# Hourglass attention and a quick-GELU MLP on one core: batch 0's values loaded by halves of the heads, the second half as fp32 over SyncE's queue

## The chip, the cores and the metric

The kernel runs on one core of a Trainium2 chip. The metric is the device time of one execution in microseconds; smaller is better. A core has five engines that run side by side, each with its own instruction stream in program order: TensorE (PE, matmuls, with its weight loads as PEld), VectorE (DVE), ScalarE (ACT), GpSimd (POOL) and SyncE (SP, which here only issues DMAs). They meet through semaphores. DMAs are issued by POOL (queue 0, which can also convert fp32 to bf16 on the way), by SP (queue 1) and once by ACT (queue 10).

## The reference

Two attentions over the same q, k, v (8 batches, 8 heads, 576 positions, head size 64), added, then an MLP with x * sigmoid(1.702 x):

```python
q_d = q.reshape(B, H, Sd, factor, D).mean(axis=3)      # factor 4; k_d, v_d alike
out_d = sm_attn(q_d, k_d, v_d)                         # softmax attention on 144 positions
out_up = np.repeat(out_d, factor, axis=2)
mask = np.abs(pos[:, None] - pos[None, :]) < factor    # local attention, 7 keys wide
out_local = np.matmul(attn, v)
x = (out_up + out_local).transpose(0, 2, 1, 3).reshape(B * S, H * D)   # 4608 x 512
h = x @ w_in                                           # 512 -> 2048
out = (h * (1.0 / (1.0 + np.exp(-1.702 * h)))) @ w_out # 2048 -> 512
```

## The kernel before, in words

The order of every engine's work is written out by hand (`manual_schedule`): instructions stand on their engine in the order in which the program issues them, and only the waits are added for it.

The MLP runs over nine groups of 512 tokens. For a group, `mm1` makes sixteen 128-row pieces (ffc 0 to 15) of h, each of four matmuls with w_in (`hps_mm`, L738), and ACT turns each into gT by Silu (L749). `mm2` multiplies gT by w_out (L808), four 128-token tiles of sixteen matmuls each, and stores. In group 0 the order of `mm2` is cut so that the late pieces of w_out come late: tiles 2, 3, 0, 1 with f 0 to 7 first (32 matmuls), then tile 0 with f 8 to 11 and f 12 to 15, and so on.

The attention of batch g + 1 is done inside group g, as steps between the matmuls of the MLP. `POS_G[0]` says ahead of which matmul of group 0 each step of batch 1 stands (numbers from 16 on count `mm2`'s matmuls), `VDP_0` the same for the selection matmuls of batch 1.

Batch 0 has nothing to hide behind, so its attention is the kernel's start. "qd" is one of two quads of four heads, "hp" one of four pairs of heads. In order:

- POOL loads k and q of both quads as bf16 (`load_1`, L183), then values: `load_vb` (L214) loads, for chunk i of five and each half of the partitions, 64 rows of all eight heads into `vbs[0]`, eight DMAs of 64 KB for chunks 0 to 3. Chunk 4 comes as fp32 by SP and ACT at the very start (`load_v`, L203) and ACT converts it (`prep_v`, L325).
- DVE transposes k and q (L261) and sums them by four positions (L304); POOL sums one of them (`pool_qk`, L315, L319). PE computes local scores (`scores`, L381, L394) and pooled ones (`scores_d`, L411); ACT takes exponents into `es` (L477) and `ed` (L483).
- `prep_vd_pe` makes the pooled values: selection matmuls (L362) with a 0/1 matrix `psel` on `vbs[0]`, all eight heads at once, fourteen of 256 columns, copied into `vd` by ACT (L371).
- `av_local0` (L499) and `av_down0` (L513, L522) are the products with the values, one pair at a time; `normalise0` on DVE (reciprocal L541, products L544 and L549) divides by the sums. Pairs 0 and 1 (the first quad) are done in two parts, pairs 2 and 3 whole (`av_whole0`).
- `turned` transposes a pair's result on PE (L564, L575) and ACT copies it into xT (L587, L591). Then the MLP's first matmuls (`part`) begin, two ffc at a time, between the transposes.
- `warm` (L606) issues matmuls without use, in gaps of PE.

POOL's stream around this matters: it holds, in order, the k and q loads of batch 0, the eight `load_vb`, w_in's first quarter, `pool_qk`, w_in's other three quarters (`load_w_in`, L237), k and q of batch 1, two pieces of w_out (`load_w_out`, L246), batch 1's values, and later the rest of w_out. A DMA issue waits for the landing of the DMA eight issues earlier, whose semaphore it takes over; POOL waits there with everything behind it.

Of the kernel before, what the change touches and what calls it, by code (L numbers as in the profile page):

```python
# [8 lines left out]
FP32 = mybir.dt.float32  # L9
# [10 lines left out]
def kernel(  # L20
# [9 lines left out]
    nc = tc.nc  # L30
    B, H, S, D = q.shape
    SD = S // 4
    HP = H // 2
    NQ = H // 4
# [6 lines left out]
    KSTART = (0, 56)  # L41
# [8 lines left out]
    ldp = ctx.enter_context(tc.tile_pool(name="loads", bufs=1))  # L50
# [11 lines left out]
    vbs = [persist.tile([128, 5, H, 65], BF16, name=f"vb{i}") for i in range(2)]  # L62
# [7 lines left out]
    PM = [psum.tile([128, 512], FP32, name=f"pm{i}") for i in range(2)]  # L70
    turn = {"m": 0}

    def pm_tile():
        turn["m"] += 1
        return PM[turn["m"] % 2]

    wz = consts.tile([128, 512], BF16, name="wz")
    wf = consts.tile([128, 512], FP32, name="wf")
# [98 lines left out]
    qf, kf, vf = {}, {}, {}  # L177
# [15 lines left out]
        load_1("k", k, kf, b, qd)  # L193
        load_1("q", q, qf, b, qd)

    def load_v(b, gate=None, chunks=range(5), queues=(nc.sync, nc.sync)):
        t = ldp.tile([128, 5, H, D], FP32, name="vf", tag="vf")
        vf[b] = t
        if gate is not None:
            gate(t[0:1, 0, 0, 0:1])  # L200
        for i in chunks:
            for par in range(2):
                queues[par].dma_start(  # L203
                    out=t[64 * par : 64 * par + 64, i],
                    in_=bass.AP(
                        tensor=v.tensor,
                        offset=v[b, 0].offset + (114 * i + KSTART[par]) * D,
                        ap=[[D, 64], [S * D, H], [1, D]],
                    ),
                )  # L210

    def load_vb(b, i):
        for par in range(2):
            nc.gpsimd.dma_start(  # L214
                out=vbs[b % 2][64 * par : 64 * par + 64, i, :, 0:D],
                in_=bass.AP(
                    tensor=v.tensor,
                    offset=v[b, 0].offset + (114 * i + KSTART[par]) * D,
                    ap=[[D, 64], [S * D, H], [1, D]],
                ),  # L220
            )

# [13 lines left out]
    def load_w_in(c, n):  # L236
        nc.gpsimd.dma_start(  # L237
            out=w_in_bf[:, :, c : c + n],
            in_=bass.AP(
                tensor=moe_w_in.tensor, offset=moe_w_in.offset + c,  # L240
                ap=[[d_ff, 128], [128 * d_ff, n_dmc], [1, n]],
            ),
        )
# [51 lines left out]
    def new_qdT(b, qd):  # L295
        t = work.tile([128, SD, 2], BF16, name=f"qdT{qd}", tag=f"qdT{qd}", bufs=1)
        qdT[b, qd] = t
        return t

    def reduce_qk(b, qd, name):  # L300
        t = kdT[qd][:, 0:SD, :] if name == "k" else new_qdT(b, qd)
        src = (kT if name == "k" else qT)[b, qd]
        with nc.allow_low_precision("the sum is rounded once, as the pairwise one is"):
            nc.vector.tensor_reduce(  # L304
                out=t, in_=src.rearrange("p (j f) a -> p j a f", f=4),
                axis=mybir.AxisListType.X, op=ALU.add,
            )

    def pool_qk(b, qd, names="kq"):
        for name, src in (("k", kT), ("q", qT)):  # L310
            if name not in names:
                continue
            sv = src[b, qd].rearrange("p (j f) a -> p j f a", f=4)
            t1 = work.tile([128, SD, 2, 2], FP32, name="pq", tag="pq")
            nc.gpsimd.tensor_tensor(  # L315
                out=t1, in0=sv[:, :, 0:2, :], in1=sv[:, :, 2:4, :], op=ALU.add
            )
            dst = kdT[qd][:, 0:SD, :] if name == "k" else new_qdT(b, qd)
            nc.gpsimd.tensor_tensor(  # L319
                out=dst, in0=t1[:, :, 0, :], in1=t1[:, :, 1, :], op=ALU.add  # L320
            )

    def prep_v(b, eng, i=slice(0, 5), h=slice(0, H)):
        cp = eng.copy if eng is nc.scalar else eng.tensor_copy
        cp(out=vbs[b % 2][:, i, h, 0:D], in_=vf[b][:, i, h])  # L325
# [22 lines left out]
    def flat(p):  # L348
        return p.rearrange("p x n -> p (x n)")

    def prep_vd_pe(b, pv, kcs=range(3), between=None):
        n = HP
        vb, vd = vbs[b % 2], vds[b % 2]
        for kc, iis in ((0, (0, 1)), (1, (1, 2, 3)), (2, (3, 4))):
            if kc not in kcs:
                continue
            c0 = 256 * (kc - kcs[0])
            if between and kc == 1:
                between()
            for i in iis:  # L360
                for j in range(2):
                    nc.tensor.matmul(  # L362
                        pv[64 * j : 64 * j + 64, c0 : c0 + D * n],
                        lhsT=psel[:, PSEL.index((i, kc)), :],
                        rhs=sub(
                            vb[:, i], 65 * (2 * j if b else j), (4 * 65, NQ), (65 * (1 if b else 2), 2), (1, D)
                        ),
                        start=(i == iis[0]), stop=(i == iis[-1]),
                        tile_position=(0, 64 * j),
                    )  # L370
        nc.scalar.copy(  # L371
            out=vd[:, kcs[0] : kcs[-1] + 1, :, 0:D],
            in_=pv[:, 0 : 256 * len(kcs)].rearrange(
                "p (k h d) -> p k h d", k=len(kcs), h=HP
            ),
        )


# [103 lines left out]
    def exp_down(qd, sd):  # L482
        nc.scalar.activation(  # L483
            out=eds[qd][:, :, 0:432], in_=sd[:, :, 0:432],
            func=AF.Exp, scale=inv_sqrt_d / 16.0,
        )
# [50 lines left out]
    def normalise0(o, y, u, parts="ab"):  # L537
        yl, yd, rc = y
        ov = o[:, :, 0:455].rearrange("p x (c e) -> p x c e", e=65)
        c0, c1 = {"a": (0, 4), "b": (4, 7), "ab": (0, 7)}[parts]  # L540
        nc.vector.reciprocal(rc[:, :, c0:c1], ov[:, :, c0:c1, 64:65])  # L541
        if "b" in parts:
            st = 2 - u
            nc.vector.tensor_tensor(  # L544
                out=yd.rearrange("p s x d -> p x s d"), in0=ov[:, :, 4 + u : 7 : st, 0:D],
                in1=rc[:, :, 4 + u : 7 : st].to_broadcast([128, 2, 2, D]), op=ALU.mult,
            )
            c1 = 6
        nc.vector.tensor_tensor(  # L549
            out=yl[:, :, c0:c1], in0=ov[:, :, c0:c1, 0:D],  # L550
            in1=rc[:, :, c0:c1].to_broadcast([128, 2, c1 - c0, D]), op=ALU.mult,
        )
# [42 lines left out]
    def sub(t, off, *dims):  # L595
        return bass.AP(
            tensor=t.tensor, offset=t.offset + off,
            ap=[list(t.ap[0])] + [list(d) for d in dims],
        )
# [3 lines left out]
    def warm(n, cols=512, t=None, z=wz):  # L603
        t = pm_tile() if t is None else t
        for _ in range(n):
            nc.tensor.matmul(  # L606
                t[:, 0:cols], lhsT=z[:, 0:128], rhs=z[:, 0:cols], start=True, stop=True
            )
# [227 lines left out]
            f()  # L836

    POS = [13, 16, 34, 44, 58, 65]
    POS_G = {0: [16, 18, 29, 42, 56, 65], 1: [13, 16, 35, 44, 58, 65]}
    VDP_0 = 34  # L840

    o, y, x = {}, {}, {}

# [9 lines left out]
    iota_psel()  # L853
    fill()
    for i in range(4):
        load_vb(0, i)
    load_w_in(0, 512)
    warm(3, z=wf)
    warm(5, 256)
    make_off()  # L860
    make_ident(di)
    make_psel()
# [8 lines left out]
    prep_1("k", 0, 1)  # L871
    prep_1("q", 0, 1)
    reduce_qk(0, 0, "q")
    pool_qk(0, 1, "q")
    reduce_qk(0, 1, "k")
    for c in range(1, 4):
        load_w_in(512 * c, 512)
    for qd in range(NQ):
        load_qk(1, qd)
    load_w_out(0)  # L880
    load_w_out(4)
    warm(2, z=wf)
    sp = scores(0, 1, PA[0:2])
    exp_local(1, sp)
    exp_down(0, scores_d(0, 0, PA[2]))
    for hp in range(4):
        o[hp] = PA[hp % 3]
        y[hp] = y_tiles0()
    warm(1, z=wf)
    prep_vd_pe(0, PM[0], range(0, 2))  # L890
    for hp in range(2):
        av_local0(hp, o[hp], range(5))
        normalise0(o[hp], y[hp], hp % 2, "a")
    prep_vd_pe(0, PM[1], range(2, 3))
    exp_down(1, scores_d(0, 1, PA[2]))
    nc.scalar.preload_act_table_set("silu_and_others")
    for hp in range(2):
        if hp == 1:
            warm(1, t=PM[0])
        av_down0(hp, o[hp])  # L900
        normalise0(o[hp], y[hp], hp % 2, "b")

    gT0 = new_gT()
    acc = PM + [PA[n][:, u, :] for n in (1, 2, 0) for u in range(2)]
# [7 lines left out]
    def av_whole0(hp):  # L912
        av_local0(hp, o[hp], range(5))
        av_down0(hp, o[hp])
        normalise0(o[hp], y[hp], hp % 2)
# [4 lines left out]
        copy_x(0, hp, PM if n is None else PA[n][:, :, 0:288])  # L920

    av_whole0(2)
    warm(1, t=PM[0])
    turned(0, None)
    av_whole0(3)
    turned(1, 1)
    part((0, 1), 0)
    part((0, 1), 1)
# [11 lines left out]
    for g in range(n_groups):  # L940
        b = g + 1
# [66 lines left out]
        if b < B:  # L1008
            pos = POS_G.get(g, POS)
            for n, f in zip(pos, attention(b)):  # L1010
                steps.setdefault(n, []).append(f)
            if g == 0:
                steps.setdefault(VDP_0, []).append(lambda: prep_vd_pe(1, flat(PA[1])))
            if g and b + 1 < B:
# [42 lines left out]
```

## Time and profile before

| What | us |
|---|---|
| Median of three runs (308.45 to 309.1) | 308.53 |
| The profiled execution | 308.58 |
| Its span, first to last instruction | 306.8 |
| PE busy in the span | 298.0 |
| PE busy from 6 to 16 us, of 10 | 8.05 |
| PE busy from 16 to 24 us, of 8 | 6.42 |
| PE busy from 24 to 58 us, of 34 | 33.93 |
| First `load_vb` issued | 4.96 |
| First MLP matmul (L738) starts | 23.18 |
| First w_out matmul (L808) starts | 39.60 |

All later numbers are microseconds from the start of the span, of this one execution. A line of the timeline has the start, the busy time, the engine, the source line, the operation, output <- input with shapes, the count, and in brackets how long the engine stood idle before and what released it. A line of the chain of waits has start, time and what ran or was waited for; "issue" is time for which the profile shows no wait. A line of the DMA issues ends with the size of one and the time from issue to landing.

### The profile page before, as it was taken

The numbers are of one execution on the slowest core, as the hardware profiler recorded it, in microseconds if no ns is written. First come the engines' busy times: TensorE is split into PE (matmuls) and PEld (weight loads), VectorE is DVE, ScalarE is ACT, GpSimd is POOL, SyncE is SP. The second block draws the span as 40 slices with busy tenths as digits, with TensorE's granted clock in tenths as the row PEclk, the third lists the DMA queues.
The fourth block names the chain that finished last, engine by engine and source line by source line (L and its number), as shares of the span: only waits on it lengthen the run. The fifth ranks groups of instructions, "written<-read, shape, count | busy, mean of one in ns | idle before, by whom it ended". The sixth has DMA issues, their size and how long they took to land.

```text
span 306.8 us, 8494 instructions
## 1 busy us (share of the span) xinstructions
PE 298.0 (97%) x3551; PEld 147.8 (48%) x3551; DVE 187.1 (61%) x354; ACT 212.9 (69%) x351; POOL 178.9 (58%) x217
## 2 busy tenths in 40 slices
PE   7879999999999999999999999999999999999995
PEld 3455455444554455445544554455444544444444
DVE  6865523966999689886897689777975430000000
ACT  5545887867887788668966896689769876226511
POOL 8855792599698968976797669845983300000000
PEclk9999999999999999999999999999999999999999
DMA  7999999999899969826973598425101110010012
GB/s 147 152 203 209 173 132 213 177 221 215 177 230 188 188 133 226 219 46 113 232 211 66 88 218 232 84 77 150 72 0 37 36 71 0 34 71 34 0 68 71
DMA packets 64662, 40.01 MB, mean 130 GB/s; under 512 B 44656, under 2 KB 56048, under 8 KB 64624
## 3 DMA queue, kind: packets, MB, share of 16 engines
q0 software_dynamic: 18352, 14.81, 35.8%
q1 hardware_dynamic: 45600, 24.46, 32.3%
q8 instruction: 28, 0.46, 0.6%
q10 hardware_dynamic: 672, 0.20, 0.3%
q14 instruction: 10, 0.08, 0.1%
HBM read 44.83 MB, written 9.44 MB: 177 GB/s over the span
## 4 chain that ended last, share of the span: by engine, by line
PE 93%; DMA 4%; issue 1%; POOL 1%; DVE 0%; ACT 0%; POOLq 0%; DVEq 0%
PE pm L808 40%; PE pm L738 36%; PE pa L681 5%; PE pa L738 5%; DMA qb<-in_q_dram 2%; DMA vb<-in_v_dram 2%; PE pa L449 2%; PE pm L824 1%; PE pa L458 1%; PE pa L394 1%; PE pa L411 0%; POOL kb L183 0%; PE pa L513 0%; PE pa L362 0%; PE pa L499 0%
## 5 line engine op out<-in xcount | busy, mean ns | idle before, releaser
L808 PE MATMUL pm<-w_out_bf,gT 128*128 128x512 bf16 x560 | 126.2, 379 | 0.0
L738 PE MATMUL pm<-xT,w_in_bf 128*128 128x512 bf16 x512 | 119.2, 379 | 0.3 <-ACT xT L591 0.3
L749 ACT ACTIVATE gT<-pm 128x512 bf16<-128x512 f32 x128 | 76.3, 598 | 42.7 <-PE pm L738 42.7
L738 PEld LDWEIGHTS <-w_in_bf 128*128 128x128 bf16 x576 | 55.6, 98 | 67.2 <-issue 0.6
L808 PEld LDWEIGHTS <-gT 128*128 128x128 bf16 x560 | 52.9, 98 | 62.2 <-issue 0.4
L699 DVE TENSOR_TENSOR xT<-pa,r 128x300 bf16<-128x300 f32 (+3 forms) x112 | 28.0, 303 | 18.6 <-ACT r L694 17.8
L787 ACT ACTIVATE osb<-pm 128x512 f32<-128x512 f32 (+2 forms) x37 | 21.5, 580 | 24.1 <-PE pm L808 21.3
L708 POOL TENSOR_TENSOR xT<-xT,ydt 128x576 bf16<-128x576 bf16 x14 | 16.2, 1173 | 31.1 <-DVE xT L699 31.1
L789 DVE TENSOR_SCALAR osb<-pm 128x128 f32<-128x128 f32 x1 | 0.3, 292 | 55.5 <-ACT osb L787 55.5
L491 DVE TENSOR_TENSOR es<-es,mask 128x600 bf16<-128x600 bf16 x28 | 19.0, 708 | 21.2 <-ACT es L477 20.9
L693 ACT ACTIVATE r<-pa 128x504 f32<-128x504 f32 (+1 forms) x42 | 24.0, 571 | 8.4 <-PE pa L681 8.4
L694 ACT ACTIVATE r<-r 128x504 f32<-128x504 f32 (+1 forms) x42 | 25.9, 616 | 1.3
L339 POOL TENSOR_TENSOR v<-v 112x512 f32<-112x512 f32 x18 | 23.5, 1306 | 0.4
L277 DVE TENSOR_REDUCE kT<-kT 32x576 bf16<-32x576 bf16 x22 | 17.5, 795 | 8.7 <-POOL odd L272 8.3
L261 DVE STREAM_TRANSPOSE kT<-kb 128x576 f32<-128x576 f32 x16 | 20.0, 1252 | 3.4 <-DMA kb<-in_k_dram 3.1
L477 ACT ACTIVATE es<-pa 128x600 bf16<-128x600 f32 x32 | 19.7, 668 | 3.4 <-PE pa L394 3.2
L261 DVE STREAM_TRANSPOSE qT<-qb 128x576 f32<-128x576 f32 x16 | 19.8, 1238 | 0.7 <-DMA qb<-in_q_dram 0.3
L738 PE MATMUL pa<-xT,w_in_bf 128*128 128x512 bf16 x64 | 20.0, 379 | 0.0
L315 POOL TENSOR_TENSOR pq<-qT 128x576 f32<-128x576 bf16 x14 | 16.0, 1145 | 6.8 <-DVE qT L277 6.6
L277 DVE TENSOR_REDUCE kT<-odd 32x576 bf16<-32x576 bf16 x22 | 17.5, 795 | 0.7
L277 DVE TENSOR_REDUCE qT<-qT 32x576 bf16<-32x576 bf16 x22 | 17.5, 795 | 0.7
L277 DVE TENSOR_REDUCE qT<-odd 32x576 bf16<-32x576 bf16 x22 | 17.4, 791 | 0.7
(107 smaller groups left out, 344.2 us busy)
## 6 DMA issues: line engine op xcount, KB each, us to landing
out_dram<-osb SPq DMA_DIRECT2D x35, 256.0 KB, 3.2
vf<-in_v_dram SPq DMA_DIRECT2D x61, 128.0 KB, 4.3
v<-in_v_dram SPq DMA_DIRECT2D x72, 96.0 KB, 4.2
kb<-in_k_dram POOLq DMA_DIRECT2D x16, 288.0 KB, 7.1
qb<-in_q_dram POOLq DMA_DIRECT2D x16, 288.0 KB, 9.4
w_in_bf<-in_moe_w_in_dram POOLq DMA_DIRECT2D x4, 512.0 KB, 7.5
w_out_bf<-in_moe_w_out_dram POOLq DMA_DIRECT2D x3, 512.0 KB, 15.6
vb<-in_v_dram POOLq DMA_DIRECT2D x18, 64.0 KB, 6.3
```

Source lines behind the costliest of these rows:

```text
L261: nc.vector.transpose(out=t32.rearrange("p (i c) -> p c i", c=18), in_=store[b, qd].bitcast(FP32).rearrange("p (c d) -> p c d", c=18),)
L277: nc.vector.tensor_reduce(out=dst, in_=src[:, :, None], axis=mybir.AxisListType.X, op=ALU.add)
L339: eng.tensor_tensor(out=t1[0:112], in0=x[:, :, 0:2, :], in1=x[:, :, 2:4, :], op=ALU.add)
L477: nc.scalar.activation(out=es[2 * qd + u][:, :, 0:300], in_=sp[u][:, :, 0:300], func=AF.Exp, scale=inv_sqrt_d,)
L491: nc.vector.tensor_tensor(out=ev, in0=ev, in1=mask, op=ALU.mult)
L693: nc.scalar.activation(out=r, in_=den, func=AF.Ln)
L694: nc.scalar.activation(out=r, in_=r, func=AF.Exp, scale=-1.0)
L699: nc.vector.tensor_tensor(out=sub(x[u], t0 + at, (114, n), (1, c)), in0=sub(src, c0, (60, n), (1, c)), in1=sub(rc, c0, (60, n), (1, c)), o ...
L738: nc.tensor.matmul(acc, lhsT=w_in_bf[:, dmc, ffc * 128 : (ffc + 1) * 128], rhs=xT[dmc][:, g * TG : g * TG + TG], start=(dmc == 0), stop=(d ...
L749: nc.scalar.activation(out=gT[:, ffc, :], in_=acc, func=AF.Silu, scale=GELU_SCALE)
L787: eng.activation(out=osb, in_=ap, func=AF.Copy, scale=1.0 / GELU_SCALE)
L808: nc.tensor.matmul(ops[t], lhsT=gT[:, ffc, t * 128 : (t + 1) * 128], rhs=w_out_bf[:, ffc, :], start=(ffc % run == 0), stop=(ffc % run == r ...
```

## The change

Batch 0's values for chunks 0 to 3 are cut by heads. Heads 0 to 3 (the first quad) still come by POOL's queue as bf16 (`load_vb` with n=4). Heads 4 to 7 come as fp32 by SP's queue (`load_v` with h0=4), eight DMAs, which SP may issue once a memset on POOL, between the seventh and the eighth `load_vb`, has been done; POOL then converts them in two casts (`prep_v`), which stand in its stream after `pool_qk` and ahead of w_in's last three quarters. The first quarter of w_in moves behind the first addition of `pool_qk`.

`prep_vd_pe` works on one quad for batch 0: fourteen matmuls of 128 columns each time. The first quad's stand ahead of its AV; the second's stand after the first quad's AV and norms, ahead of pairs 2 and 3, and pairs 2 and 3 both come ahead of the first transposes. Five warm-up matmuls of 256 columns, two fp32 and two of 512 columns are taken out. For batch 1, the selection matmuls move from position 34 to 37 and the two AV steps from 42 and 56 to 44 and 58.

```diff
+    def load_v(b, gate=None, chunks=range(5), queues=(nc.sync, nc.sync), h0=0):
+        if h0 == 0:
+            vf[b] = ldp.tile([128, 5, H, D], FP32, name="vf", tag="vf")
+        t = vf[b]
         if gate is not None:
-            gate(t[0:1, 0, 0, 0:1])
+            gate(t[0:1, 0, h0, 0:1])
...
-                    out=t[64 * par : 64 * par + 64, i],
+                    out=t[64 * par : 64 * par + 64, i, h0:H],
...
-    def load_vb(b, i):
-        for par in range(2):
+    def load_vb(b, i, pars=(0, 1), n=H):
+        for par in pars:
...
-                out=vbs[b % 2][64 * par : 64 * par + 64, i, :, 0:D],
+                out=vbs[b % 2][64 * par : 64 * par + 64, i, 0:n, 0:D],
...
-    def pool_qk(b, qd, names="kq"):
+    def pool_qk(b, qd, names="kq", between=None):
...
+            if between:
+                between()
...
-    def prep_vd_pe(b, pv, kcs=range(3), between=None):
-        n = HP
+    def prep_vd_pe(b, pv, qd=None):
         vb, vd = vbs[b % 2], vds[b % 2]
+        if qd is None:
+            hp, dims = slice(0, HP), ((4 * 65, NQ), (65, 2))
+        else:
+            hp, dims = slice(2 * qd, 2 * qd + 2), ((2 * 65, 2),)
+        n = (hp.stop - hp.start) * D
...
-    POS_G = {0: [16, 18, 29, 42, 56, 65], 1: [13, 16, 35, 44, 58, 65]}
-    VDP_0 = 34
+    POS_G = {0: [16, 18, 29, 44, 58, 65], 1: [13, 16, 35, 44, 58, 65]}
+    VDP_0 = 37
...
     for i in range(4):
-        load_vb(0, i)
-    load_w_in(0, 512)
+        for par in range(2):
+            load_vb(0, i, (par,), 4)
+            if (i, par) == (3, 0):
+                load_v(0, gate=lambda t: nc.gpsimd.memset(t, 0.0), chunks=range(4), h0=4)
     warm(3, z=wf)
-    warm(5, 256)
...
-    pool_qk(0, 1, "q")
+    pool_qk(0, 1, "q", between=lambda: load_w_in(0, 512))
     reduce_qk(0, 1, "k")
+    for i in (0, 2):
+        prep_v(0, nc.gpsimd, slice(i, i + 2), slice(4, H))
     for c in range(1, 4):
         load_w_in(512 * c, 512)
...
-    warm(2, z=wf)
+    warm(1, z=wf)
...
-    warm(1, z=wf)
-    prep_vd_pe(0, PM[0], range(0, 2))
+    prep_vd_pe(0, PM[0], 0)
     for hp in range(2):
         av_local0(hp, o[hp], range(5))
         normalise0(o[hp], y[hp], hp % 2, "a")
-    prep_vd_pe(0, PM[1], range(2, 3))
     exp_down(1, scores_d(0, 1, PA[2]))
-    nc.scalar.preload_act_table_set("silu_and_others")
     for hp in range(2):
-        if hp == 1:
-            warm(1, t=PM[0])
         av_down0(hp, o[hp])
         normalise0(o[hp], y[hp], hp % 2, "b")
+    prep_vd_pe(0, PM[1], 1)
+    nc.scalar.preload_act_table_set("silu_and_others")
...
     av_whole0(2)
-    warm(1, t=PM[0])
+    av_whole0(3)
     turned(0, None)
-    av_whole0(3)
     turned(1, 1)
```

## The prediction, made before the result was known

> **What bounds the kernel now.** I read the page first, then the chain of waits in order of time, then the timelines of POOL and PE, and last the list of DMA issues, narrowed to one issue at a time, for landings.
>
> ```profile
> PE 298.0 (97%) x3551; PEld 147.8 (48%) x3551; DVE 187.1 (61%) x354; ACT 212.9 (69%) x351; POOL 178.9 (58%) x217
> ...
> PE   7879999999999999999999999999999999999995
> ```
>
> PE is busy for 97% of the span, and only the first three of forty slices (7.7 us each) fall short. So a change can win only by an earlier start of the unbroken stream of matmuls, and lose only by a new hole in it. Where the start goes is in the chain, from 4 us to 26 us:
>
> ```profile
> 3.87 6.09 DMA qb<-in_q_dram
> 9.96 0.28 issue
> 10.24 5.79 DMA vb<-in_v_dram
> 16.04 0.04 issue
> 16.08 0.30 PE pm L362 x2
> ...
> 20.53 1.22 issue
> 21.75 0.33 PE pm L575 x5
> ...
> 24.07 0.59 PE pm L738 x2
> ```
>
> The eighth load of values is issued only when the last q of batch 0 has landed (9.96) and lands at 16.04; selection matmuls (L362), AV and norms follow, and from 24.07 PE never stops. Two L738 matmuls ran at 23.18, so the stream might as well have begun at 24.07 - 0.43 = 23.64. The 1.22 us "issue" has no visible releaser; the DMA view of 19 to 20.5 us shows one 16 KB packet of the instruction queue just ahead of it.
>
> The other thing to read is the order on POOL, which issues all weight and k, q loads:
>
> ```profile
> 10.24 0.68 POOL L214 DMA_DIRECT2D vb<-in_v_dram  x1 [0.46 <-DMA qb<-in_q_dram]
> 11.22 0.78 POOL L237 DMA_DIRECT2D w_in_bf<-in_moe_w_in_dram  x1 [0.29 <-DMA vb<-in_v_dram]
> 12.07 1.14 POOL L315 TENSOR_TENSOR pq<-qT 128x576 f32<-128x576 bf16 x1
> 13.28 0.67 POOL L319 TENSOR_TENSOR qdT<-pq 128x288 bf16<-128x288 f32 x1
> 13.89 2.28 POOL L237 DMA_DIRECT2D w_in_bf<-in_moe_w_in_dram  x3
> ```
>
> From here to 36.9 us these loads form one unbroken train: the stretches between 16 and 34 us move 181 to 219 GB/s. w_in's second piece lands at 13.89 + 6.4 = 20.3, the third at 23.1, the fourth at 25.7, k and q of batch 1 from 27.1 in steps of 1.4, the second piece of w_out (f 4 to 7) at 20.54 + 16.4 = 36.9; batch 1's last values at 38.54 + 3.8 = 42.3 and the last piece of w_out (f 14, 15) at 40.68 + 7.9 = 48.6. PE uses that last piece first in the 13th matmul of this group:
>
> ```profile
> 48.51 3.20 PE L808 MATMUL pm<-w_out_bf,gT 128*128 128x512 bf16 x14
> ```
>
> that is at about 51.2, only 2.55 us after its landing. That number decides this forecast.
>
> **The change, part by part.**
>
> *First half of the values.* POOL still issues eight loads, but of 256 packets. Their issue takes between 0.55 (k, q: 128 packets) and 0.69 us (4.83 for seven of 512), say 0.62. The eighth still waits for q, so it is issued at 10.24. Its landing: from below, the quickest such load later needs 3.8 us for twice the bytes, so 13.7; from above, as now, 16.0. The eight loads now land over 5.1 us (10.96 to 16.04), half of which would end near 13.3; I take 14.0, nearest the floor.
>
> *PE's start.* Down scores end at 13.53; the warm-up behind them (1.12 us) is gone. Fourteen selection matmuls of 128 columns instead of 256 cost about half of 0.75 + 0.30 + 0.42, 0.7 us: done at 14.3. AV of two pairs (0.66): 14.95. DVE's reciprocal and product (0.21 + 0.69, twice) from 14.65: 16.45; the second L513 and L522 end at 17.1. The second half's selection matmuls (0.7, if POOL's casts are done) 17.8; AV, the copy of vd on ACT (between 0.38 and 0.59) and L513, L522: 19.05; the fourth pair 0.7: 19.75; two transposes of 0.7 each and the copy of xT 0.7 beside them: first L738 at 21.25. **The start gains 23.64 - 21.25 = 2.4 us.** If the 1.22 us stall comes back at its new place, 1.2. Dropping the five small matmuls and other warm-ups costs nothing if the clock holds: PE does start slow (fp32 warm-ups: six records in 4.86 us at 1.73, 0.81 each, four in 1.98 at 9.20, 0.50 each); were part of the stage to run at the slow rate again, I bound it by 1.2 us of the gain, as the stall. Both prices are covered by the waits found next.
>
> *Second half: a new wait on POOL.* The gate (a memset, 0.1) stands behind the seventh load, 4.96 + 7 x 0.62 + 0.1 = 9.4. SP then issues eight loads. A group of four at 126.91 took 2.67, 0.67 each at 512 packets; I take 0.5 at 256 (bounds 0.45 and 0.67). The last is issued at 9.5 + 3.5 = 13.0 and lands 3.1 (96 KB alone, at 64.72) to 3.7 us later (128 KB alone, at 128.27); with 3.3, **16.3**; bounds 15.7 and 17.9. Two POOL casts of 512 elements follow, 0.55 each by L329 (1.25 for 1280); the first is hidden, the second ends at 16.9.
>
> *What is queued behind that wait.* In the built order the casts stand ahead of the three w_in issues, and so of k and q of batch 1, w_out, batch 1's values. The three w_in pieces go out from 16.95, not 13.89. The one w_in piece that moved behind L315 goes out at 13.0 and still lands before 18; PE needs it at 21.25. But the train now starts with empty engines: k alone at 139.35 lands after 4.1, at the start after 4.3, and 512 KB instead of 288 KB is 2.6 instead of 1.4: 16.95 + 5.4 = 22.35 instead of 20.3. **Every later load is 2.05 us late.** w_in keeps 3 us and more of slack; batch 1's pooled q (33.2 now, 35.3 then) is there 1 us before PE asks at 36.2.
>
> *Where it meets PE,* with PE 2.4 ahead and loads 2.05 behind. w_out f 4: lands at 38.95, wanted at 40.55 - 2.4: waits 0.8. Batch 1's selection matmuls stand three matmuls later (0.65): wanted at 45.4 - 2.4, values land at 44.35: 1.35 in all. w_out f 14: wanted at 48.8, lands at 50.65: 1.85 in all, about 1.95 with wake-up. These are not added; each takes in the one before. Moving the attention step of batch 1 costs nothing: the matmuls are the same. PE's 13 more instructions are in the chain above.
>
> **Sum:** 308.58 (306.8 span and 1.78 around it; the median of the runs is 308.53) - 2.4 + 1.95 = **308.1 to 308.2; I say 308.2**. The gain is min(2.4, 2.55 - lateness), so the start's size hardly matters and every microsecond of the second half's landing counts one to one: 307.6 at the early bound, 309.7 at the late one.
>
> **Rivals.**
>
> *The loads catch up* (faster). Between 36 and 45 us the train moves only 90 to 139 GB/s, so some lateness could vanish there, or be less from the outset because engines held up by instruction fetches now idle together. With half of it gone (1.0), the gain is 1.5: 307.1; with none left, 2.4: 306.2. Against it: POOL issues those loads only on landings of earlier ones (37.21 follows 36.9), which shifts along.
>
> *SP's queue is pushed aside* (slower). Place: the wait of the second cast. A value load on SP beside k and q loads took 11.2 us at 91.31; here it runs beside the first half's loads and w_in's first piece. From a landing at 16.7 the lateness is 2.45 and the gain is gone; at 17.9, 309.7. For it: w_in's first piece now starts while SP's last loads flow. Against it: POOL's packets in flight then are small and few.
>
> *The first half does not come sooner,* since SP's packets share the same engines. Then AV starts at 16.1 as now, the start gains about 0.4 from shorter work, and the second half lands near 16.3 as well: 308.2 to 308.6. The first loads speak against it: SP's and ACT's 128 KB, side by side, landed after 3.9 and 3.5 us, hardly more than 3.7 alone. The Trainium skill, DMA: Bandwidth & Descriptors, section Issuing engines are not separate DMA queues, says that loads from different engines run on the same 16 DMA engines and interleave, and that spreading them saves only issue time. By that rule this rival is right; the trace, at that small load, agrees only in part.
>
> **How the numbers follow.** Forecast 0.42, with its own range 307.6 to 309.0: mostly within 0.2% (0.62 us, about what a measurement of this kernel can tell from no change), 0.30, else 0.08 faster and 0.04 slower. Catching up 0.26, all faster. SP late 0.25, all slower. No earlier first half 0.07: 0.04 same, 0.03 slower. Faster 0.34, same 0.34, slower 0.32. The range takes in the bounds 307.6 and 309.7 and half of the catching up: 307.0 to 309.8.
>
> **What would show it.** First L362 near 13.6 and L499 near 14.4; first L738 near 21.3; POOL's second cast ending near 17 and w_in's second issue right behind it; w_in's second piece landing near 22.4; PE holes in front of L806 (the old L808) near 38 and 49 and in front of batch 1's selection matmuls near 43, with DMA named as releaser. No holes there and a span shorter by 1 us or more would say that the loads caught up; a second cast after 17.5 is SP's rival; a first L362 group that ends at 16 is the third. The forecast is wrong altogether if the start itself gains under 0.4 us.

## The result: 316.0 us, slower

The changed kernel takes 316.0 us (median of 4 runs, 315.47 to 317.59) against 308.81 us (4 runs beside it): a ratio of 1.0241, 95% interval 1.0203 to 1.0279. The profiled execution took 315.47 us with a span of 313.0 us. The forecast was 308.2 with a range that ended at 309.8. Some executions of a kernel are disturbed, that is slower throughout at a lower clock, and every ratio here leaves them out, so that it is not always the ratio of the medians.

The page of the changed kernel. Before, PE's busy share was 97%, three slices fell short and the granted clock was 9 in every slice:

```profile
PE 295.3 (94%) x3513; PEld 149.0 (48%) x3554; DVE 187.8 (60%) x354; ACT 213.0 (68%) x351; POOL 180.2 (58%) x220
...
PE   6749999899999999999999999999999999999995
...
PEclk9775999999999999999999999999999999999999
```

PE has a hole in the third slice (15.7 to 23.5 us), and in slices 2 to 4 the chip granted less than the full clock. Behind 31 us only the eighth slice (54.8 to 62.6 us) is less full than before. So what was lost was lost in the first fifth of the time. The chain of waits (start, length, what) says how:

```profile
9.59 0.28 issue
9.88 0.61 POOL vb L215
10.49 0.04 issue
10.53 0.10 POOL vf L857
10.64 0.60 SPq L204
...
15.42 5.70 DMA vf<-in_v_dram
21.15 0.08 issue
21.23 0.56 POOL vb L328
21.79 5.49 DMA w_in_bf<-in_moe_w_in_dram
27.28 0.28 issue
27.57 17.23 DMA w_out_bf<-in_moe_w_out_dram
...
48.55 8.24 DMA w_out_bf<-in_moe_w_out_dram
56.80 0.04 issue
56.84 1.02 PE pm L806 x4
```

(The changed kernel's lines stand 2 lower than before's from L738 on: L806 is the old L808, L736 the old L738; L364, L497, L511 and L520 are L362, L499, L513 and L522.) This is the path that the prediction drew, in its order: the seventh value load, the gate, SP's eight issues, the last landing (15.42 + 5.70 = 21.12), the second cast, w_in's second piece (27.28), the last piece of w_out (56.80), L806. Only the times are others: 21.1 and not 16.3 for the landing.

Two readings of this chain need the timeline of PE beside it (start, busy time, instruction, and in brackets the wait ahead of it):

```profile
9.53 0.93 PE L392 MATMUL pa<-qT,kT 32*64 32x60 bf16 x80 [2.38 <-DVE qT L262]
...
14.55 0.59 PE L364 MATMUL pm<-vb,psel 128*64 128x128 bf16 x14
15.07 0.72 PE L497 MATMUL pa<-vb,es 64*64 64x65 bf16 x40
...
21.90 0.64 PE L364 MATMUL pm<-vb,psel 128*64 128x128 bf16 x8 [3.65 <-POOL vb L328]
...
31.53 1.89 PE L736 MATMUL pa<-xT,w_in_bf 128*128 128x512 bf16 x8
```

First, the 8.24 us in the chain are the time of a transfer and not a wait of PE: the view of PE's waits gives 0.9 us in all for L806 behind w_out. PE was late by itself. The last row, the first unbroken group of eight L736 matmuls, stood at 26.87 before: the stream started **4.66 us later**, and the last copy of the output comes **6.17 us later**. The timeline of the kernel before has for that group

```profile
26.87 1.89 PE L738 MATMUL pa<-xT,w_in_bf 128*128 128x512 bf16 x8
```

and the two chains end with that copy, first before, then changed:

```profile
303.71 0.29 DVE osb L789
...
309.88 0.29 DVE osb L787
```

Second, PE stood for 3.65 us for POOL's cast, and after that its matmuls are slow: L364 takes 0.64 us for eight where fourteen took 0.59. The view by stretches of time (stretch, length, then busy time of PE, PEld, DVE, ACT, POOL with instructions, granted clock, DMA share, GB/s) shows it:

```profile
18.00:20.00 2.00, 0.25 (x6) 0.14 (x5) 1.25 (x5) 0.00 (x0) 0.00 (x0) 0.89 1.09 193
20.00:22.00 2.00, 0.10 (x3) 0.10 (x4) 0.00 (x0) 0.00 (x0) 0.77 (x2) 0.50 0.05 11
22.00:24.00 2.00, 1.90 (x51) 1.32 (x54) 0.00 (x0) 1.41 (x2) 2.00 (x3) 0.50 0.32 14
```

The clock is 0.50 up to 28 us; before, it was 1.00 in every stretch. Shorter stretches of the changed kernel show when it fell:

```profile
9.20:9.40 0.20, 0.00 (x0) 0.00 (x0) 0.20 (x2) 0.00 (x0) 0.00 (x0) 0.81 1.31 206
9.40:9.60 0.20, 0.07 (x9) 0.07 (x16) 0.20 (x2) 0.00 (x0) 0.00 (x0) 0.50 1.37 178
...
19.40:19.60 0.20, 0.00 (x0) 0.00 (x0) 0.00 (x0) 0.00 (x0) 0.00 (x0) 0.91 0.92 163
19.60:19.80 0.20, 0.00 (x0) 0.00 (x0) 0.00 (x0) 0.00 (x0) 0.00 (x0) 0.50 0.73 142
```

PE's last matmul ahead of the hole ended at 17.89 + 0.36 = 18.25, so the clock fell about 1.3 us into the hole; the first time it fell about 2.2 us into the wait of 2.38 ahead of L392. The Trainium skill, TensorE: Matmul & The Clock Gate, Part 1: The HAM clock gate, states that PE falls to half rate after an idle window of about 3.4 us; in this trace it fell sooner, both times. Also to be seen in the stretches of 2 us: from 20 to 24 us the DMA engines move 11 to 14 GB/s. Hardly anything is queued, since w_in's pieces wait behind the cast until 21.79.

So three causes offered themselves. **Theory 1:** the landing of the second half, 4.8 us later than forecast, makes the loads behind the casts late, and they set the end. **Theory 2:** the clock, which falls because the change took warm-up matmuls out. **The start itself:** PE's late start, without the loads.

### The profile page after: what moved, and what is told of

Read it like the earlier page. It is cut to its first block, busy times and chain, and to the rows that moved or that the text cites. A ratio compares the mean times of both kernels' runs of the same rounds, so it can differ in the third digit from the quotient of the medians.

```text
span 313.0 us, 8476 instructions
## 1 busy us (share of the span) xinstructions
PE 295.3 (94%) x3513; PEld 149.0 (48%) x3554; DVE 187.8 (60%) x354; ACT 213.0 (68%) x351; POOL 180.2 (58%) x220
## 4 chain that ended last, share of the span: by engine, by line
PE 78%; DMA 14%; issue 2%; POOL 2%; SPq 1%; ACT 1%; DVE 0%; POOLq 0%
PE pm L806 35%; PE pm L736 33%; DMA w_out_bf<-in_moe_w_out_dram 8%; PE pa L679 4%; DMA kb<-in_k_dram 2%; PE pa L736 2%; DMA vf<-in_v_dram 2%; DMA w_in_bf<-in_moe_w_in_dram 2%; PE pa L447 2%; SPq L204 1%; PE pm L822 1%; POOL vb L215 1%; PE pa L456 1%; POOL w_out_bf L247 0%; ACT r L692 0%
## 5 line engine op out<-in xcount | busy, mean ns | idle before, releaser
L806 PE MATMUL pm<-w_out_bf,gT 128*128 128x512 bf16 x536 | 121.6, 380 | 4.7 <-issue 3.3
L736 PE MATMUL pm<-xT,w_in_bf 128*128 128x512 bf16 x496 | 118.9, 381 | 1.2 <-ACT xT L589 0.3
L736 PEld LDWEIGHTS <-w_in_bf 128*128 128x128 bf16 x576 | 55.7, 98 | 67.5 <-issue 1.2
L806 PEld LDWEIGHTS <-gT 128*128 128x128 bf16 x560 | 52.8, 98 | 63.8 <-issue 2.0
L697 DVE TENSOR_TENSOR xT<-pa,r 128x300 bf16<-128x300 f32 (+3 forms) x112 | 28.1, 303 | 19.7 <-ACT r L692 18.7
L342 POOL TENSOR_TENSOR v<-v 112x512 f32<-112x512 f32 x18 | 23.8, 1322 | 0.4
L475 ACT ACTIVATE es<-pa 128x600 bf16<-128x600 f32 x32 | 19.7, 668 | 4.8 <-PE pa L392 4.6
L736 PE MATMUL pa<-xT,w_in_bf 128*128 128x512 bf16 x63 | 20.1, 388 | 0.0
```

What stands on the lines that cost most here:

```text
L342: eng.tensor_tensor(out=t1[0:112], in0=x[:, :, 0:2, :], in1=x[:, :, 2:4, :], op=ALU.add)
L475: nc.scalar.activation(out=es[2 * qd + u][:, :, 0:300], in_=sp[u][:, :, 0:300], func=AF.Exp, scale=inv_sqrt_d,)
L697: nc.vector.tensor_tensor(out=sub(x[u], t0 + at, (114, n), (1, c)), in0=sub(src, c0, (60, n), (1, c)), in1=sub(rc, c0, (60, n), (1, c)), o ...
L736: nc.tensor.matmul(acc, lhsT=w_in_bf[:, dmc, ffc * 128 : (ffc + 1) * 128], rhs=xT[dmc][:, g * TG : g * TG + TG], start=(dmc == 0), stop=(d ...
L806: nc.tensor.matmul(ops[t], lhsT=gT[:, ffc, t * 128 : (t + 1) * 128], rhs=w_out_bf[:, ffc, :], start=(ffc % run == 0), stop=(ffc % run == r ...
```

## The experiments

The table has for each kernel, from its profiled execution: the end of the second cast (the second half is ready), the start of the first unbroken group of L736, and the start of the last output copy, the latter two as differences to before (26.87 and 303.71); then the median and the ratio to before's runs of the same call (medians 308.8 to 309.2), with its interval.

```
kernel                         cast ends  stream  end    us      ratio (95%)
changed                        21.8       +4.7    +6.2   316.0   1.0241 (1.0203-1.0279)
1  warm-ups back               21.3       +3.3    +5.9   314.8   1.0195 (1.0156-1.0234)
2  casts behind the train      25.5       +7.3    +7.7   316.1   1.0238 (1.0197-1.0278)
3  gate early                  16.6       +1.1    +2.0   311.0   1.0056 (1.0023-1.0089)
4  before without warm-ups     -          +1.8    +3.6   312.6   1.0136 (1.0074-1.0197)
5  3 + warm-ups                16.6       +2.1    +2.6   311.3   1.0067 (1.0045-1.0089)
6  5 + casts behind w_in       17.8       +1.3    +1.8   310.6   1.0054 (1.0033-1.0075)
7  order alone                 -          +3.1    +4.5   310.9   1.0033 (1.0001-1.0066)
8  w_in's first piece behind   18.6       +0.4    +5.4   314.0   (one run)
9  6 + three bf16 warm-ups     17.9       -0.5    +0.2   310.6   1.0032 (1.0006-1.0058)
10 9 + w_in's first in front   17.9       -0.3    +0.1   309.4   1.0015 (0.9994-1.0036)
11 6 + three fp32 warm-ups     18.9       +1.7    +2.7   311.2   1.0058 (1.0030-1.0087)
12 10 + attention step back    18.1       +2.4    +2.4   309.1   0.9993 (0.9960-1.0026)
```

The opening loads are the same instructions in all of them, and yet the last q of batch 0 lands between 9.9 us (before, run 6) and 11.2 us (runs 2 and 11; 11.0 in the changed kernel). About 1 us of "stream" is therefore luck of the one execution that was profiled; the medians stand for the rest.

**1. The warm-ups put back.** The last five stand where the kernel before had none; its two of 512 columns stay out.

```
     warm(3, z=wf)
+    warm(5, 256)
-    warm(1, z=wf)          # ahead of scores(0, 1)
+    warm(2, z=wf)
+    warm(1, z=wf)          # ahead of prep_vd_pe(0, PM[0], 0)
+    warm(5, z=wf)          # ahead of prep_vd_pe(0, PM[1], 1)
```

> The changed kernel with the warm-up matmuls of before put back at their places (5, 2, 1 and 5 of them). Theory 1 (the loads queued on POOL behind the two casts are 7 to 8 us late, and PE meets them at w_out f 14): the casts end at 21.8 as now, w_in's second piece lands near 27.3, PE waits 8 us at L806 near 48.5, and the time stays within 1 us of 316. Theory 2 (the loss is the granted clock, which fell to 0.50 at 10 to 12 us and at 20 to 28 us because the warm-ups are gone): the clock stays at 1.0 from 8 us on and the time falls to 312 or below. Under theory 1 the clock may well come back too; then the hole ahead of w_out f 14 grows by as much as the start gains.

Measured: 314.8 us, clock 1.00 in every stretch, second cast at 21.3, w_in's second piece landing at 21.27 + 5.49 = 26.8. The clock came back and the time hardly moved: of 7.2 us only 1.2 went. Theory 1 comes near in the total (it had named 315 to 317); the "8 us" of waiting that it named are wrong. PE waited 1.3 us for w_out, since its own start was still 3.3 us late (five fp32 warm-ups ran to 23.1, past the cast). Since these five took PE's time, 1.2 us is the least that the clock was worth here.

**2. The casts behind the train of loads.**

```
-    for i in (0, 2):       # stood ahead of w_in 1 to 3
-        prep_v(0, nc.gpsimd, slice(i, i + 2), slice(4, H))
     for c in range(1, 4):
         load_w_in(512 * c, 512)
     for qd in range(NQ):
         load_qk(1, qd)
+    for i in (0, 2):
+        prep_v(0, nc.gpsimd, slice(i, i + 2), slice(4, H))
```

> The changed kernel with the two POOL casts of the second values moved behind w_in's last three pieces and batch 1's k and q loads, ahead of the second load of w_out; SP's issues and the warm-ups stay as changed. Theory 1 (late loads): w_in's second piece goes out near 14.5 and lands near 20.5, w_out f 14 lands near 49 to 50 and the hole of 8.2 us ahead of it goes; what is left is the late start of the stream (its effective start was about 28.5 in the changed kernel against 23.64 before, less what the clock gives back), so 311 to 313. Theory 2 (granted clock): PE's wait of 3.65 us for the casts is still there, so the clock still falls at 20 to 28 us and the time stays within 1.5 us of 316.

Measured: 316.1, no change, but on another path. w_in's second piece lands at 15.41 + 8.4 = 23.8 instead of 27.3 and PE never waits for w_out, but now the values are late, as the chain shows:

```profile
15.80 8.95 DMA vf<-in_v_dram
24.86 0.63 POOL vb L328
```

With w_in's pieces on the engines, SP's last 64 KB needed 8.95 us where 5.70 were needed with one piece ahead. The stream starts 7.3 us late and stays 7.7 late. Theory 1's number (311 to 313) missed, because it took the landing as given; the landing itself depends on what POOL has queued. Where the casts stood, either the loads or the values paid.

**3. The gate early.** SP may issue behind POOL's third value load, not the seventh:

```
-            if (i, par) == (3, 0):
+            if (i, par) == (1, 0):
```

> The changed kernel with SP's gate behind the third of POOL's value loads and not behind the seventh, that is 2.4 us sooner; nothing else moves. Theory 1 (late loads, one to one with the second half's landing): SP's last landing moves from 21.1 to 18 to 18.8, the second cast ends near 19 to 19.5, w_in's second piece and w_out f 14 come 2.4 us sooner, and the time falls by 2.4 us to 313.5 (312.5 to 314.5). If the landing is set by w_in's first piece and the other loads that stand in the DMA engines until 20.7, and not by SP's issues: the landing stays near 20.5 and the time above 315. Theory 2 (clock): PE's wait for the casts shrinks from 3.65 to about 1.3 us; the clock falls less, and the gain exceeds 2.4 us.

Measured: 311.0. SP's first issue is at 7.01 (changed kernel 10.64), the last one lands at 11.61 + 4.3 = 15.9, **5.2 us sooner**, and the time falls by **5.0 us**. That is one to one, as the prediction had it, but not by the loads alone: the stream itself starts 3.6 us sooner than in the changed kernel, since PE no longer waits for the cast, and PE waits for no load of weights. The sizes in the expectation were too small: this gate passed 3.6 us sooner, not 2.4, and with w_in's first piece behind all of SP's issues the latency is 4.3. POOL's order is now the one that was forecast for the change itself:

```profile
16.07 0.62 POOL L328 CAST vb<-vf 128x512 bf16<-128x512 f32 x1 [0.39 <-DMA vf<-in_v_dram]
16.62 2.28 POOL L238 DMA_DIRECT2D w_in_bf<-in_moe_w_in_dram  x3
```

(16.95 was forecast), and w_in's second piece lands at 16.62 + 5.8 = 22.4 (22.35). Yet the time is 311.0 and not 308.2. The clock is 0.50 again, from 18 to 24 us. That rest is what runs 5 to 7 and 9 to 12 look for.

**4. The kernel before without the warm-ups.** The same removals as in 1, and `warm(1, t=PM[0])` twice, in the kernel before.

> The kernel before without the same warm-up matmuls; no load, queue or order is touched. Theory 1: loads are on time, so at most the start of the stream moves: 308.5 to 309.5. Theory 2 (the clock falls because the warm-ups are gone, and that costs the 7 us): the granted clock falls to 0.50 in the stretches from 10 to 24 us, the stream of matmuls starts slow, and the time is 311 to 315.

Measured: 312.6, clock 0.57 and 0.58 from 10 to 14 us and 0.63 to 0.50 from 20 to 26. With all loads on time the warm-ups are worth 3.6 us. Of these, 1.8 are the start of the stream; the other 1.8 come later, as stops of PE (1.3 us the longest, ahead of L681) without a visible releaser, at a clock of 1.00. That these stops come from the missing warm-ups is not shown. So theory 2 is wrong for the changed kernel as it stands, where 1.2 us come back with the warm-ups, and right for the kernel before, in its start at least: a second bound, hidden under the first.

**8. What held SP's last loads up.** The changed kernel with all four w_in pieces behind the casts:

```
-    pool_qk(0, 1, "q", between=lambda: load_w_in(0, 512))
+    pool_qk(0, 1, "q")
-    for c in range(1, 4):
+    for c in range(4):
```

> The changed kernel with w_in's first piece issued behind the casts with the other three, so that only SP's and POOL's value loads are under way while the second half flows. If w_in's first piece is what took SP's last loads from an expected 3.3 to 5.7 us: the last value load lands 3.3 to 3.7 us after its issue, near 18.9, and the second cast ends near 19.5; the train then carries one piece more, so w_in's second piece still lands near 27 and the time stays at 315 to 316. If it isn't: landing near 21, second cast 21.8, w_in's second piece near 29.8 and 317.5 to 318.5.

Measured, in the chain:

```profile
14.70 3.13 DMA vf<-in_v_dram
17.94 0.62 POOL vb L328
18.56 0.73 POOL w_in_bf L238
19.29 8.02 DMA w_in_bf<-in_moe_w_in_dram
```

3.13 us for the last value load instead of 5.70: **w_in's first piece cost 2.6 us of the landing.** From SP's first issue to the last landing it is 8.2 us instead of 10.5, so 2.3; run 1, with the piece ahead as in the changed kernel, has 10.3. The Trainium skill, DMA: Bandwidth & Descriptors, section Issuing engines are not separate DMA queues, says that queues share the engines; this pair agrees. The run is also the cleanest one for theory 1. Its stream starts only 0.4 us late, 4.3 us sooner than in the changed kernel, and the end is still 5.4 us late, because w_in's second piece lands at 19.29 + 8.02 = 27.31, as in the changed kernel (27.28). PE now really stands for the loads:

```profile
PE pm L806 <- DMA w_out_bf<-in_moe_w_out_dram: 2.1, 1, 2.1
PE pm L364 <- POOL vb L328: 1.3, 1, 1.3
PE pa L409 <- POOL qdT L322: 0.7, 1, 0.7
PE pm L736 <- DMA w_in_bf<-in_moe_w_in_dram: 0.6, 1, 0.6
```

**5 and 6. The early gate with warm-ups, and the casts behind w_in's pieces too.** 5 is run 3 with `warm(5, 256)`, `warm(2, z=wf)` and `warm(1, z=wf)` at their old places; 6 moves the casts behind `load_w_in` 1 to 3, ahead of `load_qk(1, qd)`.

> The changed kernel with SP's gate behind the third value load (as in the run with the early gate) and the warm-up matmuls of before at three of their places (5, 2 and 1; the five ahead of the second half's selection matmuls stay out). Theory 1 (the loss was the landing of the second half; what is left with the early gate is the slow clock at 18 to 24 us): the second cast ends near 16.6 as with the early gate, w_in's second piece lands near 22.4, the clock stays at 1.0, the stream starts about 0.9 us ahead of before, and PE meets the loads, 2.2 us late, with nearly no hole: 308.2 (307.5 to 309.0), the time that the prediction gave for these landings. If the rest of 2 us with the early gate is not the clock but the later first half and the loads, it stays at 310 to 311.

> The run before (early gate, warm-ups) with the two POOL casts moved behind w_in's last three pieces, ahead of batch 1's k and q loads. Theory 1: SP's issues are all out by 12.3, ahead of these pieces, so the landing stays near 16 to 16.5; the casts end near 18.5, when PE is free for the second half; w_in's second piece lands near 21.3 and no more, the loads are 1 us late and not 2.2, so only the start counts: 307.5 (306.8 to 308.3). Rival (any piece of w_in on the engines holds SP's packets up, as 3.6 us when the casts were put behind the train with the late gate): the landing is 18 or later, PE waits for it, and the time is 309.5 or more.

Measured: 311.3 and 310.6; both expectations fail. The landings came as expected (cast at 16.6; 12.60 + 3.0 = 15.6 in run 6), the clock did not hold. In run 6:

```profile
16.00:18.00 2.00, 1.30 (x39) 0.87 (x28) 1.93 (x6) 0.89 (x1) 2.00 (x4) 1.00 1.23 197
18.00:20.00 2.00, 1.18 (x40) 0.80 (x40) 1.12 (x4) 1.44 (x2) 1.92 (x4) 0.92 1.09 151
20.00:22.00 2.00, 1.79 (x42) 1.30 (x43) 1.30 (x3) 0.33 (x1) 0.76 (x1) 0.50 1.19 185
```

PE was busy for 1.30 and 1.18 us of two stretches of 2 us, with no wait longer than 0.77 us, and the clock fell at 19.7 us and came back past 26 us. How full PE was does not explain this by itself. The kernel before (first line) kept its clock through four microseconds in which PE was no fuller than in run 6 (second line):

```profile
20.40:24.40 4.00, 2.48 (x55) 1.61 (x53) 2.94 (x6) 1.34 (x3) 1.45 (x2) 1.00 1.24 207
...
16.00:20.00 4.00, 2.48 (x76) 1.67 (x64) 3.05 (x9) 2.33 (x3) 3.92 (x7) 0.96 1.16 174
```

The 0.77 us is a stop ahead of L520 without a visible releaser, like the 1.22 us of before. What goes with the clock can be read from the single executions: in run 5 the two with a mean granted clock of 1.00 took 309.9 and 310.2 us, the four with 0.99 took 311.3 to 311.4; in run 6 the one with 0.998 took 309.8, the five with 0.99 took 310.6 to 310.8. So about 1 us of the rest of 2 us goes with the clock.

**7. The order alone.** The changed order of batch 0's attention with the value loads and the warm-ups (as in 5) of before.

> The changed order of the attention of batch 0 (first quad's AV and norms ahead of the second's selection matmuls) with the value loads, the place of w_in's first piece and the warm-ups of before, without SP's loads and casts. Theory 1: all loads are on time, the selection matmuls start when the eighth load lands near 16 as before, and the order gains nothing by itself: 308.3 to 309.0. If the order costs something of its own (a wait of PE for DVE's products between the quads), 309.5 or more.

Measured: 310.9, with runs from 308.0 to 313.1 and a ratio of 1.0033 (1.0001 to 1.0066). The runs fall into two groups. Four had a mean clock of 0.999 or 1.000 and took 308.0 to 308.8; the others had 0.987 to 0.994 and took 310.4 or more. All 17 executions of the kernel before beside them had 0.998 or more. In the profiled execution, the slowest of them, PE stops for 0.7 and 1.4 us without a releaser and the clock falls from 20 to 28 us. The order brings nothing by itself, and where the clock held it cost nothing either; it lost the clock in most executions, and what decides that stays open.

**9 and 11. More warm-ups in the gaps.** Run 6 with three matmuls more, bf16 (9) or fp32 (11):

```
     for hp in range(2):
+        warm(1, t=PM[0])            # 11: warm(1, z=wf, t=PM[0])
         av_down0(hp, o[hp])
         normalise0(o[hp], y[hp], hp % 2, "b")
+    warm(1, t=PM[0])
     prep_vd_pe(0, PM[1], 1)
```

> The run with early gate, warm-ups and casts behind w_in (310.6; its clock was 1.0 up to 18 us and 0.50 from 20 to 26 us), with three bf16 warm-up matmuls more: two ahead of the down AV of the first quad's pairs, one ahead of the second half's selection matmuls. If the clock is the whole rest: it stays at 1.0, the 4.5 us of matmuls that ran at half rate from 20.5 to 25.2 take 2.3 us, and the time falls by 2 to 2.6 us to 308.0 to 308.6. If the clock falls because PE stops for 0.77 us at 19.4 for its instructions, three short matmuls do not hold it: 310.3 to 311. If the clock holds but the loads, 2.2 us late, bind: about 308.5.

> The run with three more warm-ups, with fp32 matmuls (0.5 us each at full clock, from the run's own records) in the place of the three bf16 ones (0.2 us). If the clock is the rest and bf16 matmuls are too short to hold it, this one holds it at 1.0 to 28 us at a price of 0.4 to 0.9 us on PE ahead of the second half: 308.3 to 309.0. If the clock falls here too: 310.5 to 311.5.

Measured: in run 9's profile the clock stays at 1.00 and the stream starts 0.5 us ahead of before:

```profile
16.00:18.00 2.00, 1.91 (x44) 1.15 (x42) 1.90 (x6) 0.89 (x1) 2.00 (x5) 1.00 1.34 193
18.00:20.00 2.00, 1.70 (x47) 1.04 (x44) 1.42 (x5) 0.82 (x2) 2.00 (x5) 1.00 1.02 139
20.00:22.00 2.00, 1.49 (x49) 1.18 (x50) 0.85 (x3) 0.95 (x1) 0.75 (x1) 1.00 1.21 198
```

That execution took 309.1; it was the quickest of 12, and the median, 310.6, is that of run 6. Ten of the 12 had a mean clock of 0.998 or more (one of six in run 6), and they took 309.1 to 310.8. So the three matmuls hold the clock in most executions, and yet the typical time stays: the clock is the rest of 2 us in one execution, not in the typical one. Run 11 also holds the clock, in all nine executions, and gives 311.2: a fp32 warm-up is two matmuls, 1.1 us and not the 0.5 that the expectation counted, and the three of them cost more than they save.

**10 and 12. w_in's first piece in front, and batch 1's attention step put back.** 10 is run 9 with `load_w_in(0, 512)` right behind the value loads. 12 is run 10 with

```
-    POS_G = {0: [16, 18, 29, 44, 58, 65], 1: [13, 16, 35, 44, 58, 65]}
-    VDP_0 = 37
+    POS_G = {0: [16, 18, 29, 42, 56, 65], 1: [13, 16, 35, 44, 58, 65]}
+    VDP_0 = 34
```

> The same with w_in's first piece issued right behind the value loads, ahead of the two POOL sums, where the kernel before has it. It then shares the engines with SP's last three value loads: they land up to 2.5 us later, near 18, and the casts end near 18.5 to 19 where PE asks for the values at 18; against that w_in's second piece lands near 20.5 to 21 and not at 22.5, and no later load is late. With the clock held: 307.3 to 308.3, and if SP's last loads are held up as in the changed kernel (5.7 us), 309 to 310.

> The run with w_in's first piece in front (309.4; its stream of matmuls started 0.28 us ahead of before and ended 0.13 us behind it), with the attention step of batch 1 put back to where the kernel before has it (selection matmuls at 34, third group at 42). Reading to be tested: the 0.32 us that PE waits at L806 near 56 us for ACT's osb copy, which stands behind the three reciprocals L691 and L692, comes from that step standing two matmuls later, and not from the loads. Then the wait goes, and the time falls by 0.3 us to 309.1 (308.7 to 309.4), the same as before within what can be told. If batch 1's values, 1 us late, are met at the earlier place, PE waits for DMA or the selection matmuls near 45 us in its place, and the time stays at 309.4 or above.

Measured: 309.4 and 309.1. In run 10 SP's last load lands at 11.63 + 4.7 = 16.3, the forecast's number, w_in's second piece at 14.43 + 6.9 = 21.3, and PE waits for no load of weights. By the medians w_in's place is worth 1.2 us (310.6 to 309.4), though the two intervals overlap. What is left of waits behind 30 us is one:

```profile
56.38 1.89 PE L806 MATMUL pm<-w_out_bf,gT 128*128 128x512 bf16 x8 [0.32 <-ACT osb L785]
```

In run 12 it is gone; the medians (309.4 and 309.1) are too close to show the 0.3 us. There stream and end differ from before by the same 2.4 us. (Its profiled execution had a clock of 0.994 and took 311.1, as another one with 0.994 took 311.3; the nine with 0.998 to 1.000 took 308.5 to 309.8.) With the landing, the clock and the attention step mended, the change is worth nothing: 0.9993 (0.9960 to 1.0026). No version beat the kernel before.

## Why the prediction was wrong

**The step that failed: "Second half: a new wait on POOL", the landing of 16.3.** It came at 21.12. The gate stood at 10.53 and not at 9.4, because the seventh load waited for k's landing (9.59), which the count of issues left out: 1.1 us. Part of this is luck of the profiled execution: the same k landed at 8.5 in the kernel before, and in run 8, with the gate at the same place, it passed at 9.55. SP's eight issues took 0.68 us each (10.64 to 15.42) and not 0.5; half the packets do not take half the time, and the row at 126.91 us (0.67) was the right one: 1.3 us. The last load took 5.70 and not 3.3, because w_in's first piece, which the same change moves to 14.10, stood ahead of it (run 8: 3.13 without it): 2.4 us. The prediction saw this collision, under its second rival, and ended the bound at 17.9.

**What followed from it through the loads was right.** Cast and issue follow the landing by 0.67 us (0.65 forecast), w_in's second piece lands 5.49 later (5.4), every load comes late, and w_out f 14 meets PE. Run 8 shows this path nearly alone: PE starts 0.4 us late, w_in's second piece lands at 27.31 as in the changed kernel, and the end is 5.4 us late. What the prediction named as a condition ("if POOL's casts are done") and gave no price is that the same late cast holds up PE itself, for 3.65 us: a second path, nearly as late. Run 2 shows that one: w_in's second piece lands at 23.8, the values at 24.8, and the stream starts 7.3 us late. "Every microsecond of the second half's landing counts one to one" came out in run 3 (5.2 us sooner, 5.0 us faster), but there both paths got shorter at once, so the closeness of the two numbers is in part luck. The sum from 308.2 to 315.47: w_in's second piece 27.28 instead of 22.35, 4.9; the train loses 1.2 more up to w_out f 14 (56.80 instead of 50.65), for which no run looked; the wait for ACT's output copy and what else follows L806 0.4; the rest around the span 0.7 (315.47 - 313.0 against 1.78).

**"The start gains 2.4 us" failed as well,** and would have failed with the landing forecast. It took the warm-ups out and kept the clock. Run 4 gives their price with loads on time, 3.6 us, of which 1.8 in the start, where 1.2 was the bound. In run 3, with the landing at 15.9, the stream starts 1.1 us late. "Both prices are covered by the waits" is right for the kernel as changed (run 1: 1.2 us of 7.2) and for none of the better ones. With the clock held by matmuls that take PE's time, 0.5 us of the 2.4 are left at best (run 9). ("PE's 13 more instructions" is a miscount on which no price hung: the trace has 3554 weight loads against 3551.)

**The first half comes sooner** only in part. L497 began at 15.07 (14.4 forecast, 16.32 before). With the early gate it began at 15.10 and 15.40 in runs 6 and 9, and at 16.33 in run 10, where q landed late and w_in's first piece stood close behind: there it is what the third rival said.

**"Moving the attention step of batch 1 costs nothing":** PE waits 0.3 us for it. The matmuls are the same, but ACT's output copy stands behind the step's reciprocals, and with the step two matmuls later the next L806 waits for that copy (run 10; no such wait in run 12 and before).

**The rivals:** SP's queue pushed aside is what happened, in its place and by its mechanism, with 0.25 and a bound that was too near.

## What to carry to other kernels

A transfer that something will wait for is priced with what the same change puts on the DMA engines beside it, and with the wait of the instruction that gates it; its price alone on the engines is only the floor. Before matmuls that "only keep warm" are taken out, let a run show what the granted clock does without them; how full PE is around them did not tell. And where two bounds lie close, undoing one shows nothing (runs 1 and 2): read stream and end apart, and mend both.

## What was not expected of the hardware

- The clock halved about 1.3 us into a hole (changed kernel), and in run 6 with no wait above 0.77 us, with PE busy for 2.48 us of 4. The Trainium skill, TensorE: Matmul & The Clock Gate, Part 1: The HAM clock gate, names an idle window of about 3.4 us; none of these waits had lasted as long. Three matmuls of 128x512 in bf16 kept the clock in ten of 12 executions (run 9). What decides it stays open, since the kernel before kept its clock at the same 2.48 us of 4.
- SP's issue of a 64 KB load takes 0.60 to 0.79 us in the changed kernel, 0.68 from one to the next; four loads of 128 KB in the kernel before took 0.67 each. Single issues took 1.3 us (run 2) and 1.5 and 1.6 us (run 1).
- The 64 KB load that SP issued last took 3.13 us with no piece of w_in on the way (run 8), 5.70 with one issued 1.3 us ahead of it (changed kernel), and 8.95 with one ahead and three more issued from 0.4 us ahead of it on (run 2). In run 1, where SP's own issue was late and the one piece stood 3.0 us ahead, it took 3.88.
